# Eight column tiles share the first two contraction blocks of a GEGLU layer

## The chip, the core and the metric

The kernel runs on one core of a Trainium2 chip. The metric is the time of one execution on the device, in microseconds (us), over repeated executions. Each timed execution comes with its recorded span, from the first to the last instruction of the kernel, which is about 2 us shorter than the time. Moments in the text are read from single records of the traces; they agree with the printed views to 0.01 us.

## The reference

```python
B, S, D, F = 32, 32, 1024, 3584          # bf16; x has 1024 rows
def reference(x, w_gate, w_up, w_down):
    return (gelu_tanh(x @ w_gate) * (x @ w_up)) @ w_down
```

## The kernel before

A matmul multiplies a 128x128 stationary block (weights) with a 128x512 moving block (x, transposed) and adds into one of eight banks of PSUM. The F = 3584 columns are 28 tiles of 128; D = 1024 is 8 contraction blocks k. A tile needs 16 matmuls for half of the rows: 8 blocks for w_gate (j = 0), 8 for w_up (j = 1).

The kernel saves multiplications by a Strassen-like scheme (seven products of half-size blocks instead of eight). The sums of blocks which that scheme needs take time to arrive and to be computed. So the kernel starts with a plain stage: tiles 0 to 9 against the first half of the rows (160 matmuls, 4.6 to 39.9 us). Then comes the stage of fp32 products, and from about 180 us the product with w_down. Only the plain stage and its loads are changed. In it, partial sums after block k = 3 are copied out of PSUM, since the scheme uses them later ("kept").

`pr.add` records operations with the tiles they touch. The program then works out which semaphores each operation has to wait for. On TensorE the order is that of the calls; on the other engines `at` is only a sort key.

```python
# x blocks 0 and 1 come plain and are transposed on TensorE; blocks 2..7 by transposing DMAs on the sync queue
for k in range(NX):                       # NX = 2
    load_first("sp", 0, k, k + 1)         # w_gate block k of tiles 0..3, 128 KB
    load_first("act", 1, k, k + 1)        # w_up
for k0, k1 in ((2, 3), (3, 4), (4, 5), (5, 6), (6, 8)):
    load_x(0, k0, k1)
...
# tiles 0..3 together: 8 banks, k outermost, so 8 matmuls for each x block and weight block
steps = [(m, j, k) for k in range(DK - KO) for j in range(2) for m in range(4)]
for m in range(4):
    steps += [(m, j, k) for j in range(2) for k in range(DK - KO, DK)] + [(m, None, None)]
for m, j, k in steps:
    ...
    op = mm(2 * m + j, first[:, j, k, m * P:(m + 1) * P], xT[0][:, k, :], k == 0, k in (3, DK - 1), add=k > 3)
    if k == 3: ...                        # copy the bank to kept[m]: ScalarE for even m, VectorE for odd m
...
load_duo(2, 0, 10, None, 2, [begin_late]) # weights of tiles 4, 5, in two halves of k: k = 0..3, then k = 4..7
load_duo(3, 0, 11, None, 2)               # tiles 6, 7
...
for p in range(4, EARLY):                 # tiles 4..9, one after the other, two banks each
    for b, j, k0 in ((g, 0, 0), (u, 1, 0), (g, 0, 4), (u, 1, 4)):
        for k in range(k0, k0 + 4):
            mm(b, stat(p, j, k), x0[:, k, :], k == 0, k in (3, 7), add=k > 3)
        if k0 == 0:
            act(kept[p][:, j, :], bank(b), COPY, at + 0.9 * (j + 1))     # copy out after k = 3
```

## Time and profile before

| | before |
|---|---|
| median of the first three runs | 273.16 us (273.12 to 273.28) |
| span of the profiled execution | 271.2 us |
| first real matmul / full clock / first fp32 product | 4.60 / 6.30 / 39.92 us |
| last matmul | 268.77 us |

The profile's page first gives the busy time of each engine (us, share of the span, number of instructions) and the chain of work that ended last.

```profile
span 271.2 us, 3314 instructions
PE 267.6 (99%) x1197; PEld 191.8 (71%) x1206; DVE 203.5 (75%) x238; ACT 132.8 (49%) x213; POOL 37.2 (14%) x23
...
PE 99%; issue 0%; DVE 0%
```

TensorE (PE) bounds the kernel, and nothing else shows on the chain. The list of weight loads (PEld) is split wherever the engine idled. In this timeline of the kernel before, columns are start, busy time, what was loaded, count, and in brackets the idle time before it with what ended it. A weight load normally comes one matmul (0.216 us) ahead of its own matmul.

```profile
20.11 0.53 PEld L117 LDWEIGHTS ps<-arena 128*128 128x128 bf16 x3
21.02 0.56 PEld L117 LDWEIGHTS ps<-arena 128*128 128x128 bf16 x4 [0.38 <-issue]
21.88 2.29 PEld L117 LDWEIGHTS ps<-arena 128*128 128x128 bf16 x12 [0.30 <-issue]
24.48 0.55 PEld L117 LDWEIGHTS ps<-arena 128*128 128x128 bf16 x4 [0.32 <-ACT hT L117]
...
28.00 0.56 PEld L117 LDWEIGHTS ps<-arena 128*128 128x128 bf16 x4 [0.38 <-issue]
...
31.47 0.55 PEld L117 LDWEIGHTS ps<-arena 128*128 128x128 bf16 x4 [0.32 <-ACT hT L117]
```

These are the places where tiles 4 (21.02), 5 (24.48), 6 (28.00) and 7 (31.47) go on with k = 4 after ScalarE has copied the bank out. Tiles 5 and 7 wait 0.32 us for ScalarE, which their one-matmul lead just covers, so their matmuls are on time. Tiles 4 and 6 wait 0.38 us, and their matmuls start 0.079 us late.

The windows view (stretch, its length, then busy time and count for PE, PEld, DVE, ACT, POOL, then clock, DMA share, GB/s) of the plain stage:

```profile
4.50:12.00 7.50, 7.45 (x32) 3.25 (x32) 1.15 (x4) 2.19 (x5) 0.00 (x0) 1.00 1.20 248
12.00:20.00 8.00, 7.95 (x38) 3.57 (x38) 4.16 (x7) 3.48 (x7) 0.00 (x0) 1.00 1.04 290
20.00:28.00 8.00, 7.95 (x37) 3.10 (x35) 2.52 (x4) 4.18 (x7) 0.00 (x0) 1.00 1.08 182
28.00:34.00 6.00, 6.00 (x29) 2.53 (x29) 6.00 (x7) 4.66 (x7) 0.00 (x0) 1.00 1.16 302
```

The DMA engines are about fully busy, TensorE has no hole, and VectorE and ScalarE have room until 28 us. (The 0.05 us of PE missing before 12 us are a wait just ahead of the first real matmul; those missing from 12 to 28 us are records that the trace lost.)

### The profile page before, as it was taken

How to read it: one execution, taken by the hardware profiler on the slowest of the kernel's cores; microseconds unless marked ns; L12 is line 12 of the kernel's file. 1: busy time of each engine (PE TensorE's matmuls, PEld its weight loads, DVE VectorE, ACT ScalarE, POOL GpSimd, SP SyncE). 2: the span in 40 equal slices, each digit the busy share in tenths (PEclk: the TensorE clock that was granted, in tenths of full speed). 3: DMA queues.
4: the chain of work that ended last, by engine and by line, in shares of the span. 5: the costliest groups of instructions: out<-in, count | busy, mean ns of one | idle time of the engine just before them, and what ended most of it. 6: DMA issues, size and time to landing. Idle time of an engine off the chain costs nothing.

```text
span 271.2 us, 3314 instructions
## 1 busy us (share of the span) xinstructions
PE 267.6 (99%) x1197; PEld 191.8 (71%) x1206; DVE 203.5 (75%) x238; ACT 132.8 (49%) x213; POOL 37.2 (14%) x23
## 2 busy tenths in 40 slices
PE   8999999999999999999999999999999999999996
PEld 4444448888888888888776776664458888888884
DVE  1341998998899889988764739289976999999911
ACT  2335776566756675667455564531220305067452
POOL 1000003023302330234345060000000000000000
PEclk9999999999999999999999999999999999999999
DMA  7999960050492500942900070293010000002102
GB/s 189 275 282 186 276 187 4 9 147 0 120 294 53 155 0 2 282 145 65 248 0 0 0 259 14 81 347 117 0 39 19 4 0 0 0 0 80 58 19 97
DMA packets 47039, 27.46 MB, mean 101 GB/s; under 512 B 8624, under 2 KB 47024, under 8 KB 47024
## 3 DMA queue, kind: packets, MB, share of 16 engines
q1 hardware_dynamic: 44800, 25.30, 34.4%
q10 hardware_dynamic: 2224, 1.97, 2.8%
q8 instruction: 9, 0.15, 0.2%
q14 instruction: 6, 0.05, 0.1%
HBM read 23.33 MB, written 2.10 MB: 94 GB/s over the span
## 4 chain that ended last, share of the span: by engine, by line
PE 99%; issue 0%; DVE 0%
PE ps L117 99%; DVE o L117 0%
## 5 line engine op out<-in xcount | busy, mean ns | idle before, releaser
L117 PE MATMUL ps<-S,T 128*128 128x512 f32 x560 | 129.2, 391 | 0.0
L117 PEld LDWEIGHTS ps<-S,T 128*128 128x128 f32 x560 | 105.1, 188 | 22.5
L117 ACT ACTIVATE tmp<-ps 128x512 f32<-128x512 f32 x64 | 38.0, 595 | 52.2 <-PE ps L117 52.2
L117 POOL TENSOR_TENSOR T<-arena 128x1024 fp32r<-128x1024 bf16 x17 | 36.5, 2156 | 124.4 <-PE ps L117 74.2
L117 PE MATMUL ps<-T,S 128*128 128x512 f32 x224 | 51.3, 390 | 0.0
L117 DVE TENSOR_TENSOR T<-arena,T 128x1024 fp32r<-128x1024 bf16 x42 | 50.9, 1218 | 0.2
L117 PEld LDWEIGHTS ps<-T,S 128*128 128x128 f32 x224 | 42.0, 188 | 8.8
L117 DVE TENSOR_TENSOR hT<-tmp,ps 128x512 bf16<-128x512 f32 x56 | 37.2, 684 | 14.3 <-PE ps L117 11.9
L117 ACT ACTIVATE ps<-ps 128x512 f32<-128x512 f32 x44 | 25.6, 583 | 36.6 <-PE ps L117 36.6
L117 PE MATMUL ps<-arena 128*128 128x512 bf16 x186 | 42.6, 384 | 0.4
L117 DVE TENSOR_TENSOR tmp<-ps,tmp 128x512 f32<-128x512 f32 x28 | 19.4, 692 | 23.2 <-PE ps L117 23.2
L117 PEld LDWEIGHTS ps<-arena 128*128 128x128 bf16 x192 | 17.8, 98 | 24.3 <-issue 3.2
L117 DVE TENSOR_TENSOR T<-arena 128x1024 fp32r<-128x1024 bf16 x25 | 30.0, 1220 | 5.0 <-PE ps L117 4.3
L117 DVE TENSOR_TENSOR ps<-ps,tmp 128x512 f32<-128x512 f32 x32 | 22.2, 695 | 3.0 <-PE ps L117 3.0
L117 PE MATMUL ps<-arena,hT 128*128 128x512 bf16 (+2 forms) x124 | 24.3, 355 | 0.1
L117 PEld LDWEIGHTS ps<-arena,hT 128*128 128x128 bf16 x126 | 11.7, 98 | 12.7 <-issue 0.5
L117 ACT ACTIVATE tmp<-tmp 128x512 f32<-128x512 f32 x28 | 17.6, 633 | 2.4 <-DVE tmp L117 2.1
L117 DVE TENSOR_TENSOR S<-hT 128x1024 fp32r<-128x1024 bf16 x14 | 16.6, 1219 | 0.0
L117 ACT ACTIVATE T<-arena 128x1024 fp32r<-128x1024 bf16 x14 | 14.8, 1059 | 0.0
L117 ACT ACTIVATE ps<-hT 128x512 f32<-128x512 f32 x18 | 10.7, 599 | 8.0 <-DVE hT L117 8.0
L117 ACT ACTIVATE hT<-ps 128x512 f32<-128x512 f32 x14 | 8.0, 599 | 10.8 <-PE ps L117 10.8
L117 PE MATMUL ps<-S 128*128 128x512 f32 x56 | 12.9, 389 | 0.0
(32 smaller groups left out, 89.1 us busy)
## 6 DMA issues: line engine op xcount, KB each, us to landing
arena<-in_w_down_dram SPq DMA_DIRECT2D x4, 1792.0 KB, 8.8
arena<-in_w_gate_dram SPq DMA_DIRECT2D x10, 512.0 KB, 4.0
arena<-in_w_up_dram SPq DMA_DIRECT2D x10, 512.0 KB, 5.4
out_dram<-arena SPq DMA_DIRECT2D x12, 128.0 KB, 1.7
arena<-in_w_gate_dram SPq DMA_DIRECT2D x4, 256.0 KB, 5.0
arena<-in_w_up_dram SPq DMA_DIRECT2D x4, 256.0 KB, 5.1
arena<-in_w_up_dram ACTq DMA_DIRECT2D x4, 128.0 KB, 4.0
arena<-in_w_gate_dram ACTq DMA_DIRECT2D x2, 256.0 KB, 4.0
```

What stands on the lines that cost most here:

```text
L117: ins = name(eng, *args, **kw) if callable(name) else getattr(eng, name)(*args, **kw)
```

## The change

In the plain stage before, each x block is used by 8 matmuls (1.73 us) and then the next one must be there. The change lets eight tiles share the first two blocks. Tiles 0 to 3 do k = 0, 1 and their partial sums go to SBUF. Tiles 4 to 7 run whole. Then tiles 0 to 3 get their sums back and go on in twos. So x block 2 is due 16 matmuls (3.46 us) later than before. The price is more copies between PSUM and SBUF. Tiles 4 to 7 no longer hand over one bank pair at a time.

```diff
+        for q in range(2):                       # weights of tiles 0..3 and of tiles 4..7, blocks 0 and 1
+            for k in range(NX):
+                load_quad("sp", q, 0, k, k + 1)
+                load_quad("act", q, 1, k, k + 1)
 ...
+        for k in range(NX):                      # tiles 0..3, blocks 0 and 1
+            for j in range(2):
+                for m in range(4):
+                    raw(m, j, k, 2 * m + j, k == 0)
+                    if k == NX - 1:
+                        copy(("act", "dve")[m % 2], kept[m][:, j, :], bank(2 * m + j), 6.5 + 0.9 * j + 0.1 * m)
 ...
+            begin_late = raw(4 + m, j, k, 2 * m + j, k == 0)     # tiles 4..7 whole, k outermost
             if k == 3:
+                copy(("act", "dve")[m % 2], kept[4 + m][:, j, :], bank(2 * m + j), 14.5)
 ...
+        for m in (0, 2):                         # tiles 0, 1, then 2, 3: sums back, then blocks 2..7
+            at = 21.9 + 2.59 * m
+            four = [(n, j) for n in (m, m + 1) for j in range(2)]
+            for n, j in four:
+                copy(("act", "dve")[j], bank(2 * n + j), kept[n][:, j, :], ...)
+            for k0, k1 in ((NX, 4), (4, DK)):
+                for n, j in four:
+                    for k in range(k0, k1):
+                        raw(n, j, k, 2 * n + j, False)
+                    if k1 == 4:
+                        copy("act", kept[n][:, j, :], bank(2 * n + j), at + 0.6 + 0.43 * (2 * (n - m) + j))
+                    elif j == 1:
+                        raw_done(n, 2 * n, at + 2.7 + 1.73 * (n - m))
 ...
-        load_duo(2, 0, 10, None, 2, [begin_late])
-        load_duo(3, 0, 11, None, 2)
 ...
-        for p in range(4, EARLY):
+        for p in range(8, EARLY):
 ...
-            ... (5, 5, 0), (7, 5, 1) ...
+            ... (7, 5, 0), (7, 5, 1) ...         # group 5's left weights are loaded two tiles later
```

More of the change, by code (lines that the diff above doesn't have):

```diff
@@ L162, in bass_standalone__geglu_ffn__sampling_kernel @@
         xT = [arena[:, a:a + 4096].rearrange("p (k n) -> p k n", n=512) for a in (16384, 0)]
-        first = arena[:, 20480:28672].rearrange("p (j k c) -> p j k c", j=2, k=DK)
+        quad = [arena[:, a:a + 8192].rearrange("p (j k c) -> p j k c", j=2, k=DK) for a in (20480, 8192)]
         def duo(a): return arena[:, a:a + 4096].rearrange("p (j k c) -> p j k c", j=2, k=DK)
@@ L205, in bass_standalone__geglu_ffn__sampling_kernel, with load_quad @@
             dma(eng, xn[:, 2 * i:2 * i + 2, :], x_r[:, 2 * i:2 * i + 2, 0:NX * P], 0, f"xn{i}")
-        def load_first(eng, j, k0, k1, after=()):
-            dma(eng, first[:, j, k0:k1, :], w_r[j][:, k0:k1, 0:4 * P], 0, f"w0_{j}_{k0}", after)
-        def load_x(h, k0, k1, after=()):
-            pr.add("sp", "dma_start_transpose", xT[h][:, k0:k1, :], xf[h * 512:(h + 1) * 512, k0 * P:k1 * P],
-                   dma=f"x{k0}_{h}", after=after)
-        for k in range(NX):
-            load_first("sp", 0, k, k + 1)
-            load_first("act", 1, k, k + 1)
+        def load_quad(eng, q, j, k0, k1, at=0, after=()):
+            dma(eng, quad[q][:, j, k0:k1, :], w_r[j][:, k0:k1, 4 * q * P:4 * (q + 1) * P], at, f"w{q}_{j}_{k0}", after)
+        for q in range(2):
+            for k in range(NX):
+                load_quad("sp", q, 0, k, k + 1)
+                load_quad("act", q, 1, k, k + 1)
         for k0, k1 in ((2, 3), (3, 4), (4, 5), (5, 6), (6, 8)):
-            load_x(0, k0, k1)
+            pr.add("sp", "dma_start_transpose", xT[0][:, k0:k1, :], xf[0:512, k0 * P:k1 * P], dma=f"x{k0}_0")
         for k in range(2, 4):
-            load_first("act", 0, k, k + 1)
-            load_first("act", 1, k, k + 1)
+            for j in range(2):
+                load_quad("act", 1, j, k, k + 1)
         act(warm[:, 0:1], const0, GELU, 0)
@@ L245, in bass_standalone__geglu_ffn__sampling_kernel, with copy, raw, raw_done @@
         base = t0
+        bank = lambda b: ps[:, b, :]
+        def copy(eng, out, a, at):
+            if eng == "act":
+                act(out, a, COPY, at)
+            else:
+                pr.add("dve", "tensor_copy", out, a, at=at)
+        x0, x1 = xT
+        def raw(m, j, k, b, start):
+            return mm(b, quad[m // 4][:, j, k, m % 4 * P:(m % 4 + 1) * P], x0[:, k, :], start, k in (NX - 1, 3, DK - 1), add=not start and k >= NX)
+        def raw_done(m, b, at):
+            act(tmp[:, m % 4, :], bank(b), GELU, at)
+            tt(hT[:, m, 0:512], tmp[:, m % 4, :], bank(b + 1), MUL, at + 0.9)
+        for k in range(NX):
+            for j in range(2):
+                for m in range(4):
+                    raw(m, j, k, 2 * m + j, k == 0)
+                    if k == NX - 1:
+                        copy(("act", "dve")[m % 2], kept[m][:, j, :], bank(2 * m + j), 6.5 + 0.9 * j + 0.1 * m)
+        for i, k in enumerate((4, 6)):
+            for j in range(2):
+                load_quad("act", 1, j, k, k + 2, 9 + i)
         KO = 2
-        bank = lambda b: ps[:, b, :]
         steps = [(m, j, k) for k in range(DK - KO) for j in range(2) for m in range(4)]
@@ L253, in bass_standalone__geglu_ffn__sampling_kernel @@
             if j is None:
-                at = 17.0 + m * 0.87
-                act(tmp[:, m, :], bank(2 * m), GELU, at)
-                tt(hT[:, m, 0:512], tmp[:, m, :], bank(2 * m + 1), MUL, at)
+                raw_done(4 + m, 2 * m, 19.4 + m * 0.87)
                 continue
-            op = mm(2 * m + j, first[:, j, k, m * P:(m + 1) * P], xT[0][:, k, :], k == 0, k in (3, DK - 1), add=k > 3)
+            begin_late = raw(4 + m, j, k, 2 * m + j, k == 0)
             if k == 3:
-                if m % 2 == 0:
-                    act(kept[m][:, j, :], bank(2 * m + j), COPY, 10.5)
-                else:
-                    pr.add("dve", "tensor_copy", kept[m][:, j, :], bank(2 * m + j), at=10.5)
@@ L264, in bass_standalone__geglu_ffn__sampling_kernel @@
-            if (m, j) == (3, 1):
-                if k < 2:
-                    load_first("act", 0, 2 * k + 4, 2 * k + 6, [op])
-                    load_first("act", 1, 2 * k + 4, 2 * k + 6)
-                if k == 3:
-                    begin_late = op
-        PLACE = [(None, 4096), (None, 0), (8192, 4096), (12288, 0), (20480, 24576), (8192, 12288), (20480, 24576)]
+                copy(("act", "dve")[m % 2], kept[4 + m][:, j, :], bank(2 * m + j), 14.5)
+            if k == 2 and m == j == 0:
+                for k0 in range(NX, DK, 2):
+                    for i in range(2):
+                        load_quad("sp", 0, i, k0, k0 + 2, 9, [begin_late] if k0 == NX and i == 0 else ())
@@ new lines, in bass_standalone__geglu_ffn__sampling_kernel @@
+        for m in (0, 2):
+            at = 21.9 + 2.59 * m
+            four = [(n, j) for n in (m, m + 1) for j in range(2)]
+            for n, j in four:
+                copy(("act", "dve")[j], bank(2 * n + j), kept[n][:, j, :], at - 1.5 + 0.8 * (n - m) if m == 0 else at - 2)
+            for k0, k1 in ((NX, 4), (4, DK)):
[6 more added lines that the diff above has]
+                        raw_done(n, 2 * n, at + 2.7 + 1.73 * (n - m))
@@ L275, in bass_standalone__geglu_ffn__sampling_kernel, with load_duo @@
+        PLACE = [(None, 4096), (None, 0), (None, 4096), (None, 0), (20480, 24576), (8192, 12288), (20480, 24576)]
         brief = tmp[:, 4:8, :].rearrange("p t n -> p (t n)").bitcast(BF16).rearrange("p (j k c) -> p j k c", j=2, k=DK)
-        def load_duo(g, s, at, place=None, parts=1, after=()):
-            m, n = 2 * g + 14 * s, DK // parts
+        def load_duo(g, s, at, place=None):
+            m = 2 * g + 14 * s
             place = duo(PLACE[g][s]) if place is None else place
-            for k in range(0, DK, n):
-                for j in range(2):
-                    dma("sp", place[:, j, k:k + n, :], w_r[j][:, k:k + n, m * P:(m + 2) * P], at, f"w{g}{s}{j}{k}", after)
-                    after = ()
@@ L285, in bass_standalone__geglu_ffn__sampling_kernel @@
-        load_duo(2, 0, 10, None, 2, [begin_late])
-        load_duo(3, 0, 11, None, 2)
+            for j in range(2):
+                dma("sp", place[:, j, :, :], w_r[j][:, :, m * P:(m + 2) * P], at, f"w{g}{s}{j}")
         for k0 in range(0, DK, 2):
@@ L298, in pair_w @@
             if a is None:
-                return first[:, :, ks, p * P:(p + 1) * P]
+                return quad[p // 4][:, :, ks, p % 4 * P:(p % 4 + 1) * P]
             return duo(a)[:, :, ks, (p % 2) * P:(p % 2 + 1) * P]
@@ L304, in sxf @@
         def sxf(s, k): return Sf[:, 4 * s + k:4 * s + k + 2, :]
-        x0, x1 = xT
         def sums_x(s, at):
@@ L338, in stat @@
             return pair_w(p, 0, slice(k, k + 1))[:, j, 0, :]
-        for p in range(4, EARLY):
+        for p in range(8, EARLY):
             at = 18.9 + (p - 4) * 3.46
-            g = (0, 2, 4, 6, 2, 0)[p - 4]
+            g = (2, 0)[p - 8]
             u = g + 1
@@ L358, in bass_standalone__geglu_ffn__sampling_kernel @@
         sums_x(3, 37.2)
-        sums_x(4, 28)
+        sums_x(4, 29.6)
         sums_w(0, 3, 36)
@@ L368, in bass_standalone__geglu_ffn__sampling_kernel @@
             A, E = ((0, 1), (2, 3)) if short or (p - EARLY) % 2 == 0 else ((2, 3), (0, 1))
-            for q, g, s in ((1, 2, 1), (3, 3, 1), (3, 4, 0), (3, 4, 1), (5, 5, 0), (7, 5, 1), (9, 6, 0), (9, 6, 1)):
+            for q, g, s in ((1, 2, 1), (3, 3, 1), (3, 4, 0), (3, 4, 1), (7, 5, 0), (7, 5, 1), (9, 6, 0), (9, 6, 1)):
                 if p == q:
```

## The prediction

> **What bounds the kernel now.** TensorE's issue of matmuls. The page has PE busy 267.6 us of 271.2 (99%), and the chain of waits is "PE ps" for 99%. Busy is not peak, so I read the starts of single matmuls in the trace. From the first real matmul at 4.60 us they lie 0.427 us apart until 6.3 us (clock record: full clock from there), then 0.216 us through the whole stretch that the change rewrites (160 matmuls, to 39.9 us). The Trainium skill ("TensorE: Matmul & The Clock Gate", Part 1) gives 426.7 ns cold and 215.7 ns warm for 512 columns; the trace agrees. I find just two real stalls, 0.08 us each (21.0 and 28.0 us), where a bank goes on with k=4 after ScalarE copied it out. Gaps of exactly 0.43 us are missing records. The first four tiles wait for no x or weight block, though the DMA share is about 1 from 2 to 34 us (windows view). So the slack that the change buys for DMA is off the critical path.
>
> **What changes.** The matmuls stay: 16+64+48+32 = 160, same shapes.
> - Data are due later: x block 2 at about 12.3 us instead of 8.9, its transpose issued only 0.9 us later (two more 0.46 us issues ahead). Second-quad blocks 0 and 1, due at 8.9 and 10.6 us, issue by 3.1 us and land some 4 us later (DMA view). The rest of quad 0, 1.5 MB, issues at about 12.5 us, due at 22.7. All in time.
> - The second-half x transposes issue about 2 us sooner (six weight DMAs ahead instead of eight).
> - ScalarE and VectorE get 8 copies more each, 0.52 to 0.62 us apiece: about 5 us of each in the first 34 us, where both are about half idle. VectorE's preparation of S and T slips by perhaps 1 us; the first T sum was ready at 37.1 us for a use at 39.9, so it still fits.
> - The eight copies after block 1, and after block 3 of tiles 4 to 7, have the eight-matmul lead (1.73 us) of the old block-3 copies; those just fitted (last copy ended at 13.72 us, its bank due at 13.85).
> - The tightest new place: ScalarE runs four GELUs and two restores (0.60 us each) from 19.9 us on, then copies out tile 0's gate bank until about 24.4 us, when PE wants it; a copy's end to the next matmul was 0.13 us at 21.0. I expect one stall of 0.05 to 0.2 us there.
> - Removed: the two 0.08 us stalls of tiles 4 and 6.
>
> **On the critical path**: -0.16 us, +0.05 to +0.2 us; about zero. Group 5's left weights, loaded at tile 7 instead of 5, still have over 15 us before their first use.
>
> **Prediction: 273.2 us, range 272.7 to 274.0.** Faster by over 2%: 1%; within 2%: 97%; slower by over 2%: 2%.
>
> **What would show it.** Matmuls 0.216 us apart from 6.3 to 40 us, first fp32 product within 0.3 us of 39.9; the two stalls gone and at most a small one near 24.4 us, released by a ScalarE copy; no PE or weight-load wait on a DMA; ACT and DVE busy up about 5 us each; the chain still 99% PE; the stretch from 40 us unchanged.
>
> **What would make it wrong.** A second-quad block late (PE waiting for arena DMA at 8.9, 10.6 or 15.8 us); ScalarE's queue order making restores late, stalls adding to 1 us or more; VectorE slipping by over 2.5 us, so that first sums are late at 40 us; DMAs crowded around tile 7 (group 5 and the first w_down block); the clock opening later than 6.3 us, at 0.21 us for each further cold matmul.

## The result, and the profile after

| | before | after |
|---|---|---|
| median of the six runs each | 273.14 us (272.63 to 273.50) | 272.63 us (272.18 to 273.15) |
| profiled span | 271.2 us | 270.9 us |
| first real matmul / full clock | 4.60 / 6.30 us | 4.60 / 6.00 us |
| first fp32 product | 39.92 us | 39.62 us |
| first fp32 product to last matmul | 228.85 us | 228.82 us |

The ratio of the times is 0.9984, 95% interval 0.9969 to 0.9999. Ratios here are the mean time of one kernel's fast runs over that of the other's of the same rounds, so not quite the ratio of the medians quoted. The median lies 0.07 us below the lower end of the predicted range. The change is well within 2%, but the prediction said "about zero" and the measured difference is about half a microsecond. Where does it come from?

The page of the changed kernel:

```profile
span 270.9 us, 3344 instructions
PE 267.8 (99%) x1206; PEld 192.5 (71%) x1206; DVE 208.1 (77%) x246; ACT 136.1 (50%) x221; POOL 37.1 (14%) x23
...
PE 99%; DVE 0%; issue 0%
```

VectorE is up 4.6 us and ScalarE 3.3 us. The windows of the plain stage:

```profile
4.50:12.00 7.50, 7.45 (x33) 3.22 (x33) 2.87 (x6) 3.55 (x6) 0.00 (x0) 1.00 1.19 255
12.00:20.00 8.00, 8.00 (x39) 3.60 (x38) 2.48 (x4) 2.34 (x5) 0.00 (x0) 1.00 1.12 318
20.00:28.00 8.00, 8.00 (x39) 3.62 (x38) 6.78 (x10) 7.18 (x14) 0.00 (x0) 1.00 1.06 241
28.00:34.00 6.00, 6.00 (x30) 2.70 (x29) 6.00 (x7) 5.06 (x9) 0.00 (x0) 1.00 0.82 224
```

The extra copies fall between 20 and 28 us, where ScalarE goes from 4.18 to 7.18 us and VectorE from 2.52 to 6.78 us, without a hole in TensorE. The weight loads of the changed kernel from 21 to 32 us are one unbroken piece:

```profile
21.04 10.89 PEld L117 LDWEIGHTS ps<-arena 128*128 128x128 bf16 x51
```

Both stalls are gone, and the one that I had predicted near 24.4 us did not come. In this pair of profiles the first fp32 product is 0.303 us earlier. Two stalls of 0.079 us make 0.158. The clock became full 0.299 us earlier; a matmul takes 0.427 us before that moment and 0.216 after, so about half, 0.15, is saved. The sum is 0.31. From there on the two traces take the same time within 0.04 us. So the pair is explained, but half of it by the clock, and 0.3 us is not 0.5. Data came earlier relative to their use, as intended: x block 2 landed 1.3 us before its first matmul in the kernel before (7.54 and 8.88 us) and 3.4 us before it in the changed one (8.83 and 12.18 us). The experiments ask three things: why those stalls were there, whether the clock's moment belongs to the change, and where the rest is.

### The profile page after: what moved, and what is told of

Same layout as the page of the kernel before. It is cut to its first block, busy times and chain, and to the rows that moved or that the text cites. A ratio compares the mean times of both kernels' runs of the same rounds, so it can differ in the third digit from the quotient of the medians.

```text
span 270.9 us, 3344 instructions
## 1 busy us (share of the span) xinstructions
PE 267.8 (99%) x1206; PEld 192.5 (71%) x1206; DVE 208.1 (77%) x246; ACT 136.1 (50%) x221; POOL 37.1 (14%) x23
## 3 DMA queue, kind: packets, MB, share of 16 engines
q10 hardware_dynamic: 2512, 2.23, 3.3%
## 4 chain that ended last, share of the span: by engine, by line
PE 99%; DVE 0%; issue 0%
PE ps L117 99%; DVE o L117 0%
## 5 line engine op out<-in xcount | busy, mean ns | idle before, releaser
L117 DVE TENSOR_TENSOR hT<-tmp,ps 128x512 bf16<-128x512 f32 x56 | 36.9, 684 | 8.7 <-PE ps L117 6.7
L117 PE MATMUL ps<-arena 128*128 128x512 bf16 x192 | 43.2, 384 | 0.0
L117 PEld LDWEIGHTS ps<-arena 128*128 128x128 bf16 x192 | 18.4, 99 | 23.4 <-issue 1.8
L117 PEld LDWEIGHTS ps<-arena,hT 128*128 128x128 bf16 x126 | 11.6, 98 | 12.8 <-issue 0.5
L117 ACT ACTIVATE ps<-hT 128x512 f32<-128x512 f32 x22 | 13.0, 599 | 7.6 <-DVE hT L117 7.6
L117 ACT ACTIVATE hT<-ps 128x512 f32<-128x512 f32 x18 | 9.5, 602 | 6.1 <-PE ps L117 6.0
```

The costliest lines, as they stand in the source:

```text
L117: ins = name(eng, *args, **kw) if callable(name) else getattr(eng, name)(*args, **kw)
```

## The experiments

Names beginning with b are made from the kernel before, those with a from the changed one. Twelve kernels ran, in three groups of four, each group on one chip. All gave correct results.

### The two kernels once more (b_again, a_again)

No edit.

> The kernel before, unchanged, once more. Theory 1 (the difference in the trace is two stalls of 0.079 us that the change removes, plus the moment at which the clock opened, 6.30 us against 6.00 us, which is chance): ratio to before 1.000 within 0.001; its profile again has the two stalls near 21.0 and 28.0 us, and its clock opens anywhere between about 5.5 and 7 us, the first fp32 product moving with it by half of that. Rival A (the change itself opens the clock sooner): the clock opens at 6.30 us again, within 0.05. Rival B (late data stall the kernel before in some executions): this profile shows, beside the two stalls, a wait on an x or weight block before 20 us.

> The changed kernel, unchanged. Theory 1: ratio to before 0.9994 (minus 0.16 us), within 0.001; no stall between 6 and 40 us; its clock opens at some other moment than 6.00 us. Rival A: it opens at 6.00 us again, within 0.05, and the ratio is 0.9989 or less (minus 0.3 us). Rival B: ratio again 0.998.

Measured: b_again 272.84 us (272.29 to 273.58), ratio 0.9995 (0.998 to 1.001). a_again 272.11 us (272.05 to 272.43), ratio 0.9967 (0.9955 to 0.998). So two sets of runs of the same kernel before agree, and the changed kernel is faster by about 0.9 us this time, more than theory 1 allows.

The profile of b_again has the two stalls, its clock opened at 6.42 us, and it has a third, new stall:

```profile
11.96 0.96 PEld L117 LDWEIGHTS ps<-arena 128*128 128x128 bf16 x5
13.46 0.98 PEld L117 LDWEIGHTS ps<-arena 128*128 128x128 bf16 x6 [0.54 <-DMA arena<-in_w_up_dram]
```

That is the w_up part of blocks 4 and 5 of the first four tiles. It landed at 13.42 us in this execution and at 12.56 in the first profile, where its weight load came at 12.98. TensorE lost 0.23 us. My prediction read the first profile as "the first four tiles wait for no x or weight block". That held for that execution and not for this one. Rival B is right at least in part.

In a_again the clock opened at 4.67 us, right at the first real matmul. That is 1.33 us earlier than in the first profile of the same kernel, so rival A falls as it was stated: the moment varies between executions of one kernel. Whether the change shifts the odds of an early opening is not shown; there are too few profiles for that. The Trainium skill says the same ("TensorE: Matmul & The Clock Gate", Part 1): the activity window runs freely and the transition point is run-variable. The page's "±500ns" is small against what these traces show (3.8 to 6.5 us). a_again has no stall between 5 and 39 us, and its first fp32 product started at 39.02 us. Its x block 2 landed at 9.26 us, for a use near 11.6. Two of its lines of weight loads reach from 9.57 to 31.97 us, with no break but the 0.27 us in the second bracket, which the one-matmul lead covers:

```profile
9.57 6.64 PEld L117 LDWEIGHTS ps<-arena 128*128 128x128 bf16 x32 [0.18 <-DVE hT L117]
16.48 15.49 PEld L117 LDWEIGHTS ps<-arena 128*128 128x128 bf16 x73 [0.27 <-DVE hT L117]
```

### One wait instead of two (b_one_wait)

```diff
-                    mm(b, stat(p, j, k), x0[:, k, :], k == 0, k in (3, 7), add=k > 3)
+                    early = [landed[p, k - 2, 4]] if p in (4, 6) and j == 1 and k in (2, 3) else []
+                    mm(b, stat(p, j, k), x0[:, k, :], k == 0, k in (3, 7), add=k > 3, after=early)
```

`landed` holds the DMAs of the k = 4 halves. This adds earlier waits and takes no ordering away; the later waits then drop out because they are already known to be met.

> The kernel before, with one edit: tiles 4 and 6 wait for the second halves of their weights two matmuls earlier, at matmuls that wait for nothing else, so that no matmul waits for both a ScalarE copy and a DMA. Theory 1 with its mechanism (the stall is the second wait, an instruction of 51 ns of its own on TensorE's queue behind a copy that ends just in time): both stalls go, first fp32 product 0.157 us earlier than in the kernel before at the same clock opening; ratio 0.9994. Rival C (what my prediction said: the copy-out ends too late for the next matmul): both stalls of about 0.08 us stay at 21.0 and 28.0 us.

Measured: 272.66 us (272.31 to 273.65), ratio 0.9991 (0.9977 to 1.0006). The time alone can't tell 0.16 us. The trace can. Weight loads of b_one_wait at tiles 4, 5, 6:

```profile
20.41 0.55 PEld L117 LDWEIGHTS ps<-arena 128*128 128x128 bf16 x4 [0.32 <-ACT hT L117]
...
23.86 0.55 PEld L117 LDWEIGHTS ps<-arena 128*128 128x128 bf16 x4 [0.32 <-ACT hT L117]
...
27.31 0.55 PEld L117 LDWEIGHTS ps<-arena 128*128 128x128 bf16 x4 [0.32 <-ACT hT L117]
```

Tiles 4 and 6 now look like tile 5, the brackets say "ACT hT" in place of "issue", and the matmuls start on time. The records around tile 4 show the mechanism (time in us; duration in ns, left out for matmuls; record):

```
before, tile 4                               b_one_wait, tile 4
20.303 598 ScalarE copies the bank out       (copy ends in time)
20.751     matmul                            20.203     matmul
20.939  51 wait instruction on TensorE       20.404  95 weight load, waits for ScalarE itself
21.015  95 weight load, waits for the DMA    20.419     matmul, 0.216 after the last
21.046     matmul, 0.295 after the last
```

In these traces a weight load carries at most one wait. Where the program asks for two, the other becomes a wait instruction of its own, 51 ns on TensorE's queue. (Such a wait instruction can itself hold two waits, as one at 12.11 us in b_late_x does.) The DMA had landed at 18.14 us, long before; but the wait for it pushed the ScalarE wait into that extra instruction. The Trainium skill states the first half of this ("Perfetto Trace Analysis", Identifying Dependency Chains): EventSemaphore instructions may be inserted ahead of an instruction that waits for several engines. The trace agrees and gives the cost: 0.079 us, where the copy ends just in time. My prediction blamed the copy alone; rival C falls.

This execution's clock opened at 4.85 us, and it also has data stalls: 0.16 us at 9.7 us (x block 3 landed at 9.93 us) and about 0.10 us near 37.5, where ScalarE's copy-out came late. The first of them, in its weight loads:

```profile
10.03 1.85 PEld L117 LDWEIGHTS ps<-arena 128*128 128x128 bf16 x10 [0.46 <-issue]
```

### The second wait put back (a_two_waits)

```diff
+                    extra = [landed[2 * (p - 8) + j]] if k == 4 else []     # second-half x transposes, landed by 27 us
-                    mm(b, stat(p, j, k), x0[:, k, :], k == 0, k in (3, 7), add=k > 3)
+                    mm(b, stat(p, j, k), x0[:, k, :], k == 0, k in (3, 7), add=k > 3, after=extra)
```

> The changed kernel, with a second wait (on a DMA that landed some 9 us before) put on the first k=4 matmul of each column half of tiles 8 and 9, which already wait for a ScalarE copy. Theory 1 with its mechanism: a stall of 0.07 to 0.08 us at tile 8 and another at tile 9 (the second half of each hides in the first's delay), so 0.15 us in all, ratio to before 1.000. Rival C: no new stall, as the wait's DMA has long landed.

Measured: 272.62 us (272.16 to 273.21), ratio 0.9986 (0.9971 to 1.0). The weight loads of a_two_waits at tiles 8 and 9:

```profile
34.00 0.56 PEld L117 LDWEIGHTS ps<-arena,tmp 128*128 128x128 bf16 x4 [0.38 <-issue]
34.87 2.29 PEld L117 LDWEIGHTS ps<-arena,tmp 128*128 128x128 bf16 x12 [0.30 <-issue]
37.53 0.56 PEld L117 LDWEIGHTS ps<-arena,tmp 128*128 128x128 bf16 x4 [0.38 <-issue]
```

The matmul gaps there are 0.294 us instead of 0.216: two new stalls of 0.078 us, as in the kernel before (0.079). In the changed kernel the same places read:

```profile
34.62 0.55 PEld L117 LDWEIGHTS ps<-arena,tmp 128*128 128x128 bf16 x4 [0.32 <-ACT hT L117]
...
38.07 0.55 PEld L117 LDWEIGHTS ps<-arena,tmp 128*128 128x128 bf16 x4 [0.32 <-ACT o L117]
```

So the mechanism works in both directions, and 0.16 us of the gain belongs to it. The timed ratio fell short of the 1.000 expected, as the rest of the gain is still there. The times alone would not show the two stalls: this run's median is 0.5 us above that of a_again, three times what the stalls cost.

### x held back in both kernels (b_late_x, a_late_x)

In both kernels the first-half x transposes wait for the first real matmul, so the first of them is issued at 5.43 us (before) and 5.29 us (changed), instead of 2.23 and 3.17 us. The issue moment is nearly the same in both; the delay is 3.2 and 2.1 us.

```diff
-        for k0, k1 in ((2, 3), (3, 4), (4, 5), (5, 6), (6, 8)):
-            load_x(0, k0, k1)
 ...
+            if (m, j, k) == (0, 0, 0):
+                for k0, k1 in ((2, 3), (3, 4), (4, 5), (5, 6), (6, 8)):
+                    load_x(0, k0, k1, [op])         # op: the first real matmul; likewise in the changed kernel
```

> The kernel before, with the x transposes of the first half held on their queue until the first real matmul is done (issue at about 5.2 instead of 2.2 us). Theory D (the change buys slack for data, and the kernel before has only about 1 us of it: x block 3 landed at 9.55 us for a use at 10.39): stalls of TensorE on x blocks, 1.5 to 2.5 us in all, ratio about 1.007. Rival (slack is large in both, or the blocks' landing does not follow their issue): no stall, ratio 1.000.

> The changed kernel with the same hold (issue at about 5.2 instead of 3.2 us). Theory D: x block 2 lands at about 11 us for a use at 12, so no stall, or under 0.3 us; ratio to before 0.998 as without the hold. Rival: it stalls like the kernel before, 1 us or more.

Measured: b_late_x 274.73 us, ratio 1.0058 (1.0043 to 1.0073). a_late_x 272.80 us, ratio 0.9984 (0.9966 to 1.0001). Weight loads of b_late_x:

```profile
6.97 2.90 PEld L117 LDWEIGHTS ps<-arena 128*128 128x128 bf16 x14
11.03 1.42 PEld L117 LDWEIGHTS ps<-arena 128*128 128x128 bf16 x8 [1.16 <-issue]
13.43 0.56 PEld L117 LDWEIGHTS ps<-arena 128*128 128x128 bf16 x4 [0.98 <-issue]
```

and of a_late_x in the same stretch:

```profile
6.33 3.77 PEld L117 LDWEIGHTS ps<-arena 128*128 128x128 bf16 x18 [0.27 <-issue]
10.37 5.56 PEld L117 LDWEIGHTS ps<-arena 128*128 128x128 bf16 x27 [0.27 <-DVE hT L117]
```

The matmul starts give the stalls: 0.86 and 0.68 us in b_late_x, none in a_late_x. Both fall where blocks 3 and 4 land (10.92 and 13.36 us). The brackets again say "issue", since the wait for x is the one in the extra instruction: a DMA wait can hide under "issue". In a_late_x x block 2 landed at 10.22 us, against 8.82 and 9.26 in the two profiles of the changed kernel, and TensorE did not notice. Theory D holds. One thing is unequal in this pair of profiles: in b_late_x matmuls already lay 0.216 us apart from 5.24 us on (it has no clock record), in a_late_x only from 6.33, so TensorE came to its blocks about half a microsecond earlier in b_late_x. That can account for part of the first stall. But the times do not hang on one execution: all four of b_late_x lie at 274.34 us or above, all four of a_late_x at 272.94 or below. The change buys slack for data, and that slack is worth time when data come late or TensorE comes early.

### Weights of tiles 4 to 7 loaded whole (b_whole)

```diff
-        load_duo(2, 0, 10, None, 2, [begin_late])
-        load_duo(3, 0, 11, None, 2)
+        load_duo(2, 0, 10, None, 1, [begin_late])
+        load_duo(3, 0, 11)
```

> The kernel before with the weights of groups 2 and 3 (tiles 4 to 7) loaded whole, in four DMAs instead of eight, so that tiles 4 and 6 have no second DMA to wait for at k=4, and 4 semaphores fewer are used (59 named ones, 63 in before, 65 in the changed kernel). Theory 1 (second wait): no stall at 21 and 28 us. Theory D: stalls on data before 20 us may show as in the repeat of before (0.22 us) and are not cured. For the time outside the span: if fewer DMAs or semaphores on the sync queue change it, the excess differs from 2.05 us; if it is set by ScalarE's DMA queue or by GpSimd's program, it stays at 2.05.

Measured: 273.15 us (272.40 to 273.80), ratio 0.9997 (0.9965 to 1.003). Stalls at tiles 4 and 6: none, as theory 1 has it. But this profile fell on an execution in which the clock was full from 3.78 us, before the first real matmul, the earliest of all. An execution with such luck should have been the fastest. It was not:

```profile
6.96 0.74 PEld L117 LDWEIGHTS ps<-arena 128*128 128x128 bf16 x4
8.51 1.42 PEld L117 LDWEIGHTS ps<-arena 128*128 128x128 bf16 x8 [0.80 <-issue]
10.53 1.42 PEld L117 LDWEIGHTS ps<-arena 128*128 128x128 bf16 x8 [0.60 <-issue]
12.26 0.56 PEld L117 LDWEIGHTS ps<-arena 128*128 128x128 bf16 x4 [0.30 <-DMA arena<-in_w_gate_dram]
```

x block 2 landed at 8.40 us and block 3 at 10.43. TensorE was due to use them at about 8.0 and 10.3, and lost 0.50 and 0.30 us. Another 0.41 us were lost near 38 us. This loss may come from the edit, which moves the issue of later loads; the two losses on x lie before the first edited load is issued (12.5 us). Near 38 us ScalarE sat on a copy of weights that the next stage needs and that landed at 36.9 us (35.7 in the first profile), so its copy-out for tile 9 came late. The first fp32 product started at 40.14 us, later than in the first profile with its clock 2.5 us later.

### Two more copies where a stall was predicted (a_act_plus2)

```diff
+                        if (n, j) == (0, 0):
+                            for _ in range(2):
+                                act(p1[:, :], tmp[:, 0, :], COPY, at + 0.59)     # p1 is not yet in use
```

> The changed kernel with two more ScalarE copies (0.49 us from start to start) just ahead of the copy-out of tile 0's gate bank, where I had predicted a stall of 0.05 to 0.2 us and none came. In the trace that copy ended 0.3 us ahead of the weight load that needs it and 0.5 us ahead of the matmul. If that slack is real, 0.98 us of extra work, of which the wait for TensorE hides some 0.1, gives one stall of 0.35 to 0.55 us near 24 us, perhaps with smaller ones after it, and no others. If the slack were larger than I read, no stall; if ScalarE were as tight as predicted, 0.9 us or more.

Measured: one execution, 272.74 us. ScalarE in the changed kernel, and then in this run:

```profile
22.59 0.60 ACT L117 ACTIVATE tmp<-ps 128x512 f32<-128x512 f32 x1
23.18 2.06 ACT L117 ACTIVATE hT<-ps 128x512 f32<-128x512 f32 x4
```

```profile
21.92 0.60 ACT L117 ACTIVATE tmp<-ps 128x512 f32<-128x512 f32 x1
22.40 1.30 ACT L117 ACTIVATE p<-tmp 128x512 f32<-128x512 f32 x2
23.61 2.04 ACT L117 ACTIVATE hT<-ps 128x512 f32<-128x512 f32 x4
```

The copy-out starts 1.69 us after the last GELU instead of 0.59, so it was delayed by 1.10 us, more than the 0.98 I had reckoned. TensorE stalled once, for 0.73 us, and nowhere else. The slack is therefore 1.10 - 0.73 = 0.37 us. The stall is larger than the 0.35 to 0.55 expected, as the delay is. My predicted stall of 0.05 to 0.2 us came from adding up the 0.60 us that each ScalarE instruction shows. In the trace, starts of successive ones lie only 0.48 to 0.52 us apart (21.08, 21.60, 22.08, 22.59): each begins before the one before it is shown to have ended.

### The time outside the span (b_pad_act, b_pad_dve, b_act_dma, a_act_less)

The time of every execution exceeds its span by nearly a constant of the kernel (spans of single executions are on record to 0.1 us): 2.01 to 2.11 us in all fast executions of the kernel before, 1.75 to 1.85 us in all executions of the changed kernel. That is 0.26 us on average which no view of the profile contains. The first thought was the fetching of instructions. The Trainium skill ("Runtime: NRT & Kernel Launch", Instruction fetch mechanics) says that an engine's instruction memory is refilled in 16 KiB blocks. The traces show 16 KB pieces on one queue and 8 KB pieces on another, and the changed kernel has one 8 KB piece more, at 259 us.

```diff
+        for _ in range(17):                                   # b_pad_act
+            act(warm[:, 1:2], const0, COPY, base + 25)
+        for _ in range(7):                                    # b_pad_dve
+            pr.add("dve", "memset", warm[:, 1:2], 0.0, at=base - 30)
```

> So far every run's time exceeds its recorded span by a constant of the kernel: 2.0 to 2.1 us for the kernel before and b_one_wait, 1.75 to 1.85 us for the changed kernel and a_two_waits. In the changed kernel one more 8 KB piece of the instruction stream is fetched inside the span, at about 259 us. This run is the kernel before with 17 very short ScalarE instructions in an idle stretch at about 200 us, so that ScalarE's program is as long as in the changed kernel (331 instructions against 329 there and 314 before). Theory F (the constant depends on where an engine's program ends, as its last piece must be fetched after the span if it was not before), for ScalarE: excess falls to about 1.79 us, and an 8 KB fetch shows near 259 us. Theory F for VectorE: excess stays at 2.05. Rival (number of semaphores or queues): stays at 2.05 here and in the VectorE run. Span unchanged by the pad, but for the clock's opening.

> The kernel before with 7 very short VectorE instructions near 150 us, so that VectorE's program has the length of the changed kernel's (381 instructions; 374 before). Theory F for VectorE: time less span falls from 2.05 to about 1.79 us and an 8 KB fetch shows near 259 us; ratio about 0.999. Theory F for ScalarE, or the rival (semaphores, queues): 2.05 us as before.

Measured: 273.39 us (ratio 1.0012, 0.9993 to 1.003) and 273.14 us (1.0002, 0.9987 to 1.0017). In b_pad_act the additional piece does come, at 259.8 us. The excess stays: 2.04 to 2.11 and 2.03 to 2.08 us. In b_pad_dve no additional piece comes. Theory F as stated is refuted for both engines.

The next two runs change only how ScalarE's weight DMAs are cut.

```diff
 # b_act_dma: two of ScalarE's DMAs cut in two          # a_act_less: two pairs of ScalarE's DMAs joined
+  for i in range(2):                                    -  for k in range(2, 4):
+      dma("act", first[:, 1, k:k + 1, 256*i:256*i+256], -      for j in range(2):
+          ...)                                          -          load_quad("act", 1, j, k, k + 1)
+  for part in (6, 7):                                   +  for j in range(2):
+      load_first("act", 1, part, part + 1)              +      load_quad("act", 1, j, 2, 4)
```

> The kernel before with two of ScalarE's weight DMAs cut in two, so that ScalarE issues 13 DMAs with 65 named semaphores, as in the changed kernel (11 and 63 in before). Theory G (the time outside the span follows ScalarE's DMAs or the number of semaphores): excess falls from 2.05 to about 1.79 us. Rival (neither): 2.05 us. Theory 1: both 0.08 us stalls stay.

> The changed kernel with blocks 2 and 3 of the second quad loaded by one DMA for each weight instead of two, so that ScalarE issues 11 DMAs with 63 named semaphores, as in before. Theory G: excess rises from 1.79 to about 2.05 us. Rival: it stays at 1.79. Span as in the changed kernel; no stall between 6 and 40 us, as these blocks land near 9 us for a use at 12.

Measured: a_act_less 272.72 us, ratio 0.9989 (0.9968 to 1.001). Its excess is 2.01 to 2.10 us, that of the kernel before, while its trace is that of the changed kernel (no stall, first fp32 product at 39.11 us with the clock full at 4.96). It even has the additional piece, at 260.7 us. b_act_dma: ratio of the fast runs 1.0006 (0.998 to 1.0032), excess 2.27 to 2.38 us, so it rose where theory G had it fall. Its profile (granted clock 0.85) is not used. (One run of the kernel before in this group took 710 us and is left out as slow.) b_whole, with four DMAs fewer on the sync queue, had 2.10 to 2.11 us.

So the constant moves by a quarter of a microsecond when only the cutting of ScalarE's DMAs is touched, in both kernels. But it follows neither their number nor that of the semaphores. What sets it stays open. It is 0.26 us of the measured difference, and it does not come from the idea of the change: a_act_less keeps the idea and does not have it. What is left there, a ratio of 0.9989, is not clear of noise.

### All profiles in one sum

Up to the first fp32 product, the traces obey one sum: 36.6 us (a constant fitted to them; 159 matmul starts 0.216 us apart, 0.03 us to the fp32 product and half of the 4.61 us before the first real matmul come to nearly the same), plus half of the moment at which the clock is full (not counted before the first real matmul), plus the stalls listed. From that product to the last matmul all fast traces take 228.82 to 228.88 us. b_late_x and a_act_plus2 have no clock record, and b_act_dma is slow; these three are left out.

| profile | clock full | stalls on second waits | stalls on late data, and what follows from them | sum | measured |
|---|---|---|---|---|---|
| before | 6.30 | 0.16 | 0 | 39.91 | 39.92 |
| b_again | 6.42 | 0.16 | 0.23 | 40.20 | 40.20 |
| b_one_wait | 4.85 | 0 | 0.26 | 39.29 | 39.32 |
| b_whole | 3.78 | 0 | 1.21 | 40.10 | 40.14 |
| b_pad_act | 6.37 | 0.16 | 0 | 39.94 | 40.01 |
| b_pad_dve | 6.48 | 0.16 | 0 | 40.00 | 40.10 |
| after | 6.00 | 0 | 0 | 39.60 | 39.62 |
| a_again | 4.67 | 0 | 0 | 38.94 | 39.02 |
| a_two_waits | 4.51 | 0.16 (put in) | 0 | 39.06 | 39.10 |
| a_act_less | 4.96 | 0 | 0 | 39.08 | 39.11 |
| a_late_x | 6.33 | 0 | 0 (x held back) | 39.77 | 39.82 |

The largest misses, 0.05 to 0.10 us, are mostly in traces whose first real matmul came later than 4.61 us: 4.67 in a_again and a_late_x, 4.71 in b_pad_act, 4.78 in b_pad_dve.

The pattern: where the clock opens late, TensorE is slow for its first microseconds and data were mostly in time in either kernel (b_again lost 0.23 us all the same). Where it opened early, the two variants of the kernel before, b_one_wait and b_whole, caught up with their data and gave part of the luck, or all of it, back. The changed kernel kept it in all three such profiles.

## Why the prediction was right or wrong

- **TensorE bounds the kernel; matmuls stay the same; from 40 us nothing changes; within 2%.** Right. The stretch after the first fp32 product takes 228.85 and 228.82 us.
- **Two stalls of 0.08 us removed.** Right in size (0.158 us). The cause given, the copy-out alone, was incomplete: b_one_wait keeps the copies and loses the stalls, a_two_waits brings them back.
- **One new stall of 0.05 to 0.2 us near 24.4 us.** Wrong. There was none, and a_act_plus2 measured 0.37 us of slack. The mis-sized term is the sum of ScalarE durations, 0.60 us each, where starts lie about 0.5 us apart.
- **VectorE and ScalarE up about 5 us each.** 4.6 and 3.3 us, off the critical path, as said. The slip of perhaps 1 us in VectorE's sums did not come: the first T sum started at 35.48 us, against 35.83 before.
- **"So the slack that the change buys for DMA is off the critical path."** This is the step that failed. It was true of the one execution that was profiled. Its clock opened late, at 6.30 us, and even so two of its blocks landed only 0.4 us (w_up, blocks 4 and 5) and 0.8 us (x block 3) ahead of their use. In other executions that slack was used up: 0.23 us lost in b_again, 0.16 us on x block 3 in b_one_wait, 0.80 us on two x blocks in b_whole. The changed kernel lost nothing to late data in any of its profiles, even with x held back.
- **The clock.** Only a later opening was named as a risk. It varies from 3.8 to 6.5 us between executions. Only what lies after the first real matmul counts, so 4.6 to 6.5 us; half of that, 0.9 us, is more than the whole effect studied, and the moment helps to decide whether the data slack matters.
- **The time.** 273.2 us predicted, 272.63 measured, against 273.14 before. Of the half microsecond, 0.16 us is second waits (shown). 0.26 us is the constant outside the span, which the prediction did not have (measured; its cause is open). The rest is small in the first rounds and differs from set to set: mean spans in the repeats' group are 271.03 us before and 270.34 us after, 0.69 us apart, but b_again, the same kernel before, averaged 270.87 there, and in the first rounds the span of the changed kernel averaged 270.93. The 30 fast spans of the kernel before in the experiments' groups average 270.97 us, and the 11 of the changed kernel, first rounds and a_again together, 270.66, so 0.3 us apart, and some 0.15 us is left beside the second waits, which is not clear of noise. Stalls on data and the luck of the clock both enter there. With so few runs, I can't say what share of a mean is which.

## What to carry to other kernels

One profile without a wait does not prove slack: compare each landing with its use, and ask what happens when the consumer comes a microsecond earlier, as with a clock that opens at a chance moment. When TensorE waits just in time for another engine, keep every other wait off that weight load; here a wait for something long done still cost an instruction in front of it, and showed as idle time released by "issue". And for differences of a few tenths of a microsecond, compare traces event by event, and check time less span, before crediting the idea of a change.

## What the Trainium skill lacked or had wrong

- "TensorE: Matmul & The Clock Gate", Part 1: gives ±500ns for the moment of full clock, but also calls it run-variable, with 6, 11 or 14 slow matmuls in runs of one kernel. Here it fell anywhere from 3.8 to 6.5 us over executions that all began their matmuls at about 0.77 us. The page's 426.7 and 215.7 ns for a matmul of 512 columns agree (0.427 and 0.216 us).
- "Perfetto Trace Analysis", Identifying Dependency Chains: says that additional waits may become instructions of their own, but no cost. Here 51 ns for the instruction and 0.079 us for the matmul behind it, and the idle time is shown as "issue".
- "Runtime: NRT & Kernel Launch" names what lies outside the kernel and says that its total depends on the DMA setup, but gives no figure for that. Here the time less the span was 1.75 to 1.85, 2.01 to 2.11 or 2.27 to 2.38 us, according to how the DMAs were cut; whether this is any of the stages that the page names is not shown. It gives 16 KiB blocks for instruction fetch; the traces have 16 KB pieces on one queue and 8 KB pieces on another.
